# Ending the second threshold search after eight rounds behind a test, with a general path on VectorE alone; transposes of the search's bounds on VectorE; four blocks to one PSUM bank in the first expert's first rows

## The chip, the cores and the metric

One Trainium2 chip, and on it one NeuronCore (core 0). The metric is the time of one execution in device microseconds (us), taken as the median of several runs. The engines are named as the profile names them: PE (TensorE, matrix products; PEld is its weight load), DVE (VectorE), ACT (ScalarE), POOL (GpSimd) and SP (SyncE, which here only starts DMAs). They run side by side. Each works through its own list of instructions strictly in order, and they wait for each other by semaphores, so an instruction that waits holds up everything behind it on its engine.

## The reference

Attention with a block-causal mask over 8 batches, 8 heads, 576 positions and 64 dimensions gives a matrix of 4608 tokens by 512. A mixture of experts follows. Its assignment is greedy over all (token, expert) pairs, the largest logit first, and every expert takes exactly `cap` = 576 tokens:

```python
logits = x @ w_gate                      # 4608 x 8
order = np.argsort(-logits.flatten())
for idx in order:
    tok, e = (int(idx) // E, int(idx) % E)
    if assigned[tok] >= 0 or counts[e] >= cap:
        continue
    assigned[tok] = e
    counts[e] += 1
...
for e in range(E):
    mask = assigned == e
    h = np.maximum(x[mask] @ w1[e], 0.0)  # 512 -> 1024
    out[mask] = h @ w2[e]                 # 1024 -> 512
```

## The kernel before

The program has two phases. Attention fills the first 337 us and leaves the tokens in DRAM (`x`, as two float16 parts) and the logits in SBUF. Then the experts follow one after the other, in the order in which they fill up.

**The search.** `route(k)` finds the k-th expert to fill up and its 576 tokens. For each expert that is left it looks for the threshold above which 576 of the tokens that prefer it lie, and the expert with the highest threshold wins. The search runs for all experts at once, in base 4: in round t three candidates lie `4.0**-t` apart above the bound `lo` that is known so far. Two are counted on DVE (L800, L801, `jk`), one on ACT (L770, `ja`, by the sum of signs). A small matmul with a 0/1 matrix (`bo`, L817, `tot`) adds the counts over the partitions. DVE compares the sums with 4608 - 576 = 4032 (L820, `sg`) and so gets the step `nw`, and from it the next candidates (L793, `cd`). There are `NS` = 14 rounds. At round `NSC` = 6 the values are shifted into a second buffer `P2` (L774, tile `m_P`), so that the last rounds search in a small remainder. Each round therefore goes DVE and ACT, then PE, then DVE.

For k = 0 the search already ends after `NX` = 4 rounds, with a test on exactness (L868 to L897): where exactly 4032 values lie below the winner's bound the remaining rounds change nothing. The general path stands behind an If (L958) in which PE, ACT, DVE and SP all branch.

`finish()` turns the bounds (column 0, 1 and their sum 2 of `CB`), which lie one expert to a partition, into rows: three float32 transposes on PE (L831 `th`, L832 `bc`, PSUM tiles of the tags "tot" and "rt"). Then DVE finds the maximum and the winner `oh` (L835 to L845), the mask `MM` of its tokens (L849 to L861) and the expert's number `eidx` (L858). `place()` adds up the masks into positions: DVE scans (L892, `SC`), PE multiplies (L903 to L907, `po`), and `invert()` makes the index list `ix` from it (PE `pe` L1005 and `ps` L1012, DVE `ixt` L1008 and `ix` L1014).

**What hangs on a search.** `eidx` lets SP load the expert's weights (`weights`, L1018, tile `raw`, 512 KB each). They are split into two float16 parts: for k < 2 the first four pieces by ACT (L1035) and DVE (L1037), all others by ACT (L1042, L1046) and POOL (L1048). `ix` lets POOL gather the token rows (`gather`, L1078, `xg`). For k = 0 they are turned by PE (L1089, `xt`) and evicted by DVE and ACT halves (L1094, L1093); for all others SP starts transposing DMAs (L1104, tile `X`).

**An expert.** `ffn(k)` has two stages on PE. The first one (`h`, L1129) makes 8 blocks of 128 hidden units, each from 12 matmuls (4 parts of the 512 inputs by 3 products of float16 parts), for the first rows (128 of 576 for k = 0, 256 otherwise) and then for the rest. Each block fills one of the four PSUM banks of the tag "g"; ACT evicts it (L1115, `HH`) and DVE makes the remainder (L1117, `HL`), and only then the bank is free. The second stage (`y`, L1155, L1159) multiplies by the second weights; ACT evicts (L1137, `yo`), and POOL scatters the rows to the output (L1145, `out_dram`). The tag "g" serves `y` too.

**What sets the order.** All of this is written by generators that a small scheduler (`Sched`) interleaves when the program is built: each `yield` names an engine, a cost in ns and the events it needs, and the scheduler picks what starts first by its own model. So a changed cost or event moves instructions on every engine from there on. The search of expert k + 1 thereby runs beside the matmuls of expert k, its `tot` matmuls strewn among `h` and `y`. `sc.busy(e, t)` tells the model that an engine is busy, `sc.ev[...]` when an event will be there.

## Time and profile before

| | us |
|---|---|
| median of 3 runs | 771.02 (770.09 to 771.24) |
| the profiled execution | 771.09 |
| its span, first to last instruction | 769.3 |
| mean granted PE clock over the span | 0.986 |

The profiled execution takes 1.8 us more than its span; that part lies outside the first and last instruction. The page lists for each engine how long it was busy, the chain of waits that ended last, and the groups of instructions by line. Answers of the trace narrow this to a stretch of time: rows of one instruction or a merged run of them with start, duration, engine, line, operation, output and input, and in brackets how long the engine stood idle before and for whom. Durations of matmuls overlap, because they are pipelined; how long one costs is the distance from start to start.

### The profile page before, as it was taken

What the parts mean: (1) busy time and instruction counts of PE and PEld (TensorE: products, weight loads), DVE (VectorE), ACT (ScalarE), POOL (GpSimd) and SP (SyncE); (2) the same over time, 40 slices, a digit from 0 to 9 for tenths busy, and PEclk for the clock granted to TensorE, in tenths of its full rate; (3) what the DMA queues carried; (4) which work ended last, traced back from release to release, by engine and by line L of the source; (5) the groups of instructions that cost most, each with busy time, mean ns of one, the idle gap of its engine ahead of it and who ended that gap; (6) DMA issues with size and microseconds to landing.
All of it is one profiled execution on the core that took longest, in us unless ns stands there. A gap on an engine that the chain in (4) does not pass through costs nothing.

```text
span 769.3 us, 19008 instructions
## 1 busy us (share of the span) xinstructions
PE 715.6 (93%) x6516; PEld 474.7 (62%) x6516; DVE 559.4 (73%) x2290; ACT 536.6 (70%) x1451; POOL 467.8 (61%) x515
## 2 busy tenths in 40 slices
PE   5879999999999999966999999999999999999997
PEld 3557776766776777743545747647567475574753
DVE  6899889997799888758988978879687693430210
ACT  5788888988898898844935869594965948393211
POOL 5888978997799876714314448293761926666001
PEclk9999999999999999986999999999999999999999
DMA  9888999999999995266229376482925719853101
GB/s 203 163 160 171 207 187 216 201 168 226 187 210 171 221 196 103 78 124 192 99 74 228 104 247 158 161 211 71 292 76 193 178 43 268 273 139 88 35 14 49
DMA packets 249122, 122.84 MB, mean 160 GB/s; under 512 B 205600, under 2 KB 232096, under 8 KB 249024
## 3 DMA queue, kind: packets, MB, share of 16 engines
q1 hardware_dynamic: 243088, 102.60, 60.2%
q0 software_dynamic: 5936, 19.01, 7.9%
q8 instruction: 52, 0.85, 0.5%
q14 instruction: 46, 0.38, 0.2%
HBM read 71.45 MB, written 18.87 MB: 117 GB/s over the span
## 4 chain that ended last, share of the span: by engine, by line
PE 40%; DMA 5%; issue 4%; POOL 3%; ACT 1%; POOLq 0%; SPq 0%; DVE 0%; ACTq 0%; DVEq 0%
PE h L1129 22%; PE y L1155 15%; DMA raw<-in_moe_w_dram 2%; PE y L1159 2%; POOL xg L1078 2%; POOL W L1048 1%; DMA X<-xg 1%; DMA out_dram<-yo,ix 1%; PE pe L1005 1%; ACT ja L770 1%; DMA xg<-x,ix 0%; PE tot L817 0%; ACT yo L1137 0%; POOL out_dram L1145 0%; ACT raw L1042 0%
## 5 line engine op out<-in xcount | busy, mean ns | idle before, releaser
L442 POOL TENSOR_TENSOR P<-P,m 128x320 f32<-128x320 f32 (+8 forms) x285 | 210.2, 773 | 46.0 <-DVE m L434 30.6
L1129 PE MATMUL h<-X,W 128*128 128x320 f16 (+3 forms) x1536 | 195.4, 286 | 1.6 <-DMA X<-xg 1.6
L1129 PEld LDWEIGHTS <-W 128*128 128x128 f16 x1536 | 141.5, 98 | 43.1 <-issue 3.7
L420 ACT ACTIVATE P<-psb,m 128x576 f32<-128x576 f32 (+8 forms) x288 | 149.7, 548 | 25.6 <-DVE m L413 17.7
L1155 PE MATMUL y<-W,HH 128*128 128x512 f16 x512 | 152.3, 379 | 0.0
L409 DVE TENSOR_REDUCE m<-psb 128x1 f32<-128x576 f32 (+8 forms) x288 | 124.9, 481 | 11.6 <-PE psb L384 11.3
L1048 POOL TENSOR_TENSOR W<-raw,W 128x1024 f16<-128x1024 f32 x56 | 118.3, 2134 | 19.7 <-ACT W L1046 17.3
L467 PE MATMUL psb<-mident,P 128*128 128x128 f32 x800 | 104.6, 278 | 10.4 <-POOL P L442 5.4
L1145 POOL DMA_INDIRECT out_dram<-yo,ix x40 | 39.2, 981 | 118.0 <-ACT yo L1137 73.0
L384 PEld LDWEIGHTS <-qT 128*64 128x64 f16 x1408 | 77.0, 111 | 42.3 <-issue 28.0
L384 PE MATMUL psb<-kT,qT 128*64 128x288 f16 (+8 forms) x704 | 90.8, 284 | 10.8 <-ACT P L420 9.5
L467 PEld LDWEIGHTS psb<-mident,P 128*128 128x128 f32 x800 | 86.3, 141 | 22.0 <-POOL P L442 8.2
L502 PE MATMUL psb<-PT,V 128*64 128x448 f32 (+5 forms) x776 | 97.2, 388 | 0.9 <-DVE PT L450 0.4
L1155 PE MATMUL y<-W,HL 128*128 128x512 f16 x256 | 97.0, 379 | 0.0
L1115 ACT ACTIVATE HH<-h 128x320 f16<-128x320 f32 (+3 forms) x128 | 52.0, 410 | 62.3 <-PE h L1129 57.1
L1078 POOL DMA_INDIRECT xg<-x,ix x40 | 40.9, 1022 | 81.4 <-DMA raw<-in_moe_w_dram 48.5
L448 ACT ACTIVATE PT<-psb 128x512 f32<-128x512 f32 (+1 forms) x165 | 82.7, 595 | 5.3 <-PE psb L467 5.0
L1117 DVE SCALAR_TENSOR_TENSOR HL<-h,HH 128x320 f16<-128x320 f32 (+3 forms) x128 | 57.3, 452 | 37.0 <-ACT HH L1115 36.6
L384 PE MATMUL psb<-kS,qT 128*64 128x288 f16 (+8 forms) x704 | 83.2, 281 | 0.4 <-DVE kS L354 0.2
L1155 PEld LDWEIGHTS <-HH 128*128 128x128 f16 x512 | 46.9, 98 | 52.9 <-issue 1.8
L1042 ACT ACTIVATE raw<-raw 128x512 f32<-128x512 f32 x112 | 67.7, 625 | 9.4 <-DMA raw<-in_moe_w_dram 9.4
L502 PEld LDWEIGHTS psb<-PT,V 128*64 128x64 f32 x776 | 49.5, 137 | 32.2 <-issue 24.3
(241 smaller groups left out, 1035.3 us busy)
## 6 DMA issues: line engine op xcount, KB each, us to landing
raw<-in_moe_w_dram SPq DMA_DIRECT2D x64, 512.0 KB, 5.3
x<-XR SPq DMA_DIRECT2D x8, 1152.0 KB, 5.6
kn<-in_k_dram SPq DMA_DIRECT2D x15, 576.0 KB, 5.0
qn<-in_q_dram SPq DMA_DIRECT2D x15, 576.0 KB, 7.2
V<-in_v_dram SPq DMA_DIRECT2D x64, 128.0 KB, 4.1
V<-in_v_dram SPq DMA_DIRECT2D x16, 64.0 KB, 3.6
xg<-x,ix POOLq DMA_INDIRECT x41, 4.5
out_dram<-yo,ix POOLq DMA_INDIRECT x40, 2.8
```

What stands on the lines that cost most here:

```text
L384: nc.tensor.matmul(out if len(K1.shape) == 2 else out.rearrange("p (r j) -> p r j", r=2), lhsT=A[:, h, 64 * i:64 * i + 64], rhs=K1, start= ...
L409: nc.vector.tensor_reduce(m[:, 0, c:c + 1], ps[:, o:o + 64 * (i + 1)] if g else s.part(ps, g, i, o), axis=AX.X if g else AX.XY, op=OP.max)
L420: nc.scalar.activation(out, in_, AF.Exp, bias=m[:, 1, c:c + 1], scale=s.ESC, accum_out=m[:, 2, c:c + 1])
L442: nc.gpsimd.tensor_tensor(sl, sl, m[:, 3, c:c + 1].to_broadcast([P, w]), op=OP.mult)
L448: s.nc.scalar.activation(out, in_, AF.Copy)
L467: nc.tensor.transpose(ps[:, a], s.Pb[n % s.NP][:, s.OFF[i] + 128 * j:s.OFF[i] + 128 * j + P], s.ident)
L502: nc.tensor.matmul(ps[64 * h:64 * h + 64, 64 * (i0 - b0):64 * (b1 - b0)], lhsT=vn[:, j, 2 * (n % 2) + h, :], rhs=pt[:, s.PTI[(j, i0)]:s.PT ...
L1042: nc.scalar.activation(raw[:,x],raw[:,x],AF.Copy,scale=s.WS)
L1048: nc.gpsimd.tensor_tensor(lw,raw,hi,op=OP.subtract)
L1117: nc.vector.scalar_tensor_tensor(HL[:,f,ts],ps,0.0,HH[:,f,ts],op0=OP.max,op1=OP.subtract)
L1129: nc.tensor.matmul(ps,lhsT=W[:,a,d,f*P:f*P+P],rhs=X[:,4*(d//2)+d%2+l,ts],start=(d==0 and n==0),stop=(d==3 and n==2))
L1155: if m<4: nc.tensor.matmul(ps,lhsT=Z[:,f,m*P:m*P+P],rhs=Y[:,a,f],start=(f==n==0),stop=(f==7 and n==2))
```

## The change

Five things are changed.

- **The second search (k = 1) ends behind a test after round eight** (`s.EX={1:8}`, rounds 0 to 7). `early()` counts once more below the reached bound (`jx`, `cx`), adds it up on PE (`wn`), and tests whether a single expert has the highest bound and exactly 4032 values lie below it. The result is loaded into a register of DVE, and DVE alone branches. Where the test fails, `general()` does the other six rounds on DVE alone, with 32 by 32 transposes in place of the matmuls, and the heads again. For k = 1 the shift into `P2` at round 6 is left out of the live rounds.
- **The heads of all searches k > 0**: the bounds are brought into rows by three 32-wide transposes on DVE (`th3`) in place of the three on PE. For k = 0 the general path keeps PE's.
- **The first expert's first 128 rows**: four blocks of hidden units share one PSUM bank (`nf=4` for both halves of the 8 blocks), in the order of the input parts, with one eviction of 512 columns on ACT and one on DVE in place of four of 128. Only the first matmul of a bank has the start flag.
- **The times of the first expert's gathers** in the scheduler's model: cost on POOL (1350, 1300, 1900, 2000, 1750) ns in place of 1350 each, and landing after (3700, 2900, 2350, 2400, 2600) ns in place of 3000 each.
- **Order**: with these costs the scheduler places the instructions anew from the first expert on, on all engines.

```diff
-        s.NS=14; s.NSC=6; s.NX=4
+        s.NS=14; s.NSC=6; s.NX=4; s.EX={1:8}
...
-                    P2=s.P2 if t==s.NSC else None
+                    P2=s.P2 if t==s.NSC and not (live and k in s.EX) else None
...
+            def heads():
+                if k:
+                    th=rp.tile([P,3,32],F32,tag="th3",name=f"th{k}"); s.th3=th
+                    yield D,300
+                    for i in (2,0,1): V.transpose(th[:,i],CB[:,i:i+1].to_broadcast([P,32]))
+                    pb,th=th[:,0:2,0:8],th[:,2,0:8]
+                else:
...
+            def general():
...
+                for t in range(s.EX[k],s.NS):
...
+                    for i in range(3):
...
+                        V.tensor_scalar(cd,lo,(i+1)*4.0**-t,None,op0=OP.add)
+                        V.tensor_scalar(jk,PBx[:,:N],cd,0.0,op0=OP.is_lt,op1=OP.add,accum_out=z[:,i:i+1])
+                    V.transpose(zt,z)
+                    V.tensor_reduce(rs,zt.rearrange("p (a e) -> p e a",e=8),axis=AX.X,op=OP.add)
+                    for b in range(4): V.tensor_copy(s4[:,b],rs[32*b:32*b+32])
+                    V.tensor_reduce(s1,s4.rearrange("p b e -> p e b"),axis=AX.X,op=OP.add)
+                    for b in range(4): V.tensor_copy(x[32*b:32*b+32].rearrange("p (a e) -> p a e",e=8),s1[:,None,:].to_broadcast([32,4,8]))
+                    V.transpose(tt,x)
...
+            def early():
+                yield D,70
+                V.tensor_scalar(CB[:,2:3],lo,nw,None,op0=OP.add)
+                yield D,429
...
+                V.tensor_scalar(jk,PB[:,:N],CB[:,2:3],0.0,op0=OP.is_lt,op1=OP.add,accum_out=cx)
+                V.tensor_scalar(lo,lo,nw,None,op0=OP.add)
+                yield T,60
...
+                nc.tensor.matmul(wn,lhsT=cx.to_broadcast([P,P]),rhs=s.bo[:,0:8],start=True,stop=True)
+                yield from heads()
...
+                yield D,250
+                V.tensor_scalar(u8,s.th3[:,2,0:8],m1[:,0:1],0.0,op0=OP.is_equal,op1=OP.add,accum_out=n1[:,0:1])
+                V.tensor_scalar(u8,oh,n1[:,0:1],1.0,op0=OP.mult,op1=OP.is_equal)
+                yield D,90
+                V.scalar_tensor_tensor(u8,wn,float(s.NT-s.CAP),u8,op0=OP.is_equal,op1=OP.mult,accum_out=n1[:,1:2])
...
+                more=s.tc.If(rv==0,preferred_fallthrough_block=False); more.__enter__()
+                general()
+                more.__exit__(None,None,None)
+                sc.busy(D,1500)
...
-                yield from rounds(0,s.NS,True)
+                yield from rounds(0,s.EX.get(k,s.NS),True)
...
-            yield G,1038 if k else 1350,('ffn',k-2),('xm',k-1,m)
+            yield G,1038 if k else (1350,1300,1900,2000,1750)[m],('ffn',k-2),('xm',k-1,m)
...
-            if k==0: sc.ev['xg',k,m]=sc.now+3000
+            if k==0: sc.ev['xg',k,m]=sc.now+(3700,2900,2350,2400,2600)[m]
...
-                nf=4 if k==0 and h==0 and f0==0 else 1
+                nf=1 if k or h else 4
...
-                    if d==0: gk=sc.gtake(); pg[f]=s.ps.tile([P,512],F32,tag="g",name=f"h{k}_{f}_{h}",bufs=4)[:,:w],gk
+                    if new: gk=sc.gtake(); pf=s.ps.tile([P,512],F32,tag="g",name=f"h{k}_{f}_{h}",bufs=4)[:,:nf*w].rearrange("p (f t) -> p f t",f=nf)
```

Three places in the order of the instructions matter below. Names: a tile's name, its expert or round, and a running number; lines are those of each kernel.

On ACT, at the opening of the first expert, before:

```order
L770 ACTIVATE ja_1_5873,cn_1_5845<-m_PB,cd_1_5846 128x324
L1093 ACTIVATE X_5764<-xt_3_5892 128x4x128
L1093 ACTIVATE X_5764<-xt_4_5916 128x4x64
L1042 ACTIVATE raw_512_0_5851<-raw_512_0_5851 128x512
L1115 ACTIVATE HH_5849<-h_0_0_5853 128x128
L770 ACTIVATE ja_2_5955,cn_2_5947<-m_PB,cd_2_5948 128x324
L1115 ACTIVATE HH_5849<-h_1_0_5878 128x128
```

The same place now:

```order
L770 ACTIVATE ja_1_5864,cn_1_5832<-m_PB,cd_1_5833 128x324
L1150 ACTIVATE X_5764<-xt_3_5888 128x4x128
L1150 ACTIVATE X_5764<-xt_4_5931 128x4x64
L770 ACTIVATE ja_2_5943,cn_2_5929<-m_PB,cd_2_5930 128x324
L1099 ACTIVATE raw_512_0_5873<-raw_512_0_5873 128x512
L1172 ACTIVATE HH_5859<-h_0_0_5869 128x4x128
```

Round 2's count `ja_2` has moved ahead of the weight piece `raw_512_0` and of the eviction of `h`.

On DVE, the end of the second search now: from the heads to the winner's mask. The rows between the two branches, which the fast case jumps over (110 instructions of `general()`), are left out.

```order
L827 STREAM_TRANSPOSE th_6203<-CB_5791 128x32 x3
L838 TENSOR_REDUCE m_5804<-th_6203 128x1
...
L1174 SCALAR_TENSOR_TENSOR HL_5860<-h_4_1_6180,HH_5859 128x448
L888 SCALAR_TENSOR_TENSOR x_6225,x_6226<-wn_6201,x_6225 128x8
L890 TENSOR_LOAD x_6226
L894 COMPARE_AND_BRANCH
L894 UNCONDITIONAL_BRANCH
...
L906 TENSOR_TENSOR sm_6424<-m_BC_660,f_5803 128x32
L907 TENSOR_TENSOR d_1_5805<-PV_5771,f_5803 128x288
L1174 SCALAR_TENSOR_TENSOR HL_5860<-h_5_1_6211,HH_5859 128x448
```

All of these stand beside the last blocks of the first expert's `h`; the loading of the register and the branches are new on DVE at this place.

On PE, where the second search's positions (`po`) are made, before (weight loads left out, a "..." for matmuls of the same tile):

```order
L1155 MATMUL y_0_6340<-W_0_5763,HL_5850 128x512
L831 MATMUL th_6386<-mident,CB_5791 128x32
L832 MATMUL bc_6385<-mident,CB_5791 128x32 x2
L1155 MATMUL y_0_6340<-W_0_5763,HH_5849 128x512
...
L903 MATMUL po_2_6449<-m_sh,m_ones 128x72
```

and now:

```order
L1187 MATMUL h_7_1_6445<-X_5764,W_0_5762 128x448
...
L960 MATMUL po_2_6487<-m_sh,m_ones 128x72
...
L961 MATMUL po_2_6487<-MM_5767,m_tri 128x72
...
L962 MATMUL po_2_6487<-SC_5768,m_ones 128x72
...
L1213 MATMUL y_0_6492<-W_0_5763,HH_5859 128x512
```

`po` has moved from the middle of `y_1` (12 groups of three matmuls into the second stage) to the seam between the last `h` and the first `y`; `th` and `bc` are gone from PE. On every engine but DVE one UNCONDITIONAL_BRANCH (line 894) marks the place of the new If.

More of the change, by code (lines that the diff above doesn't have):

```diff
@@ L837, in finish @@
                 V.scalar_tensor_tensor(f[:,0],th,m1[:,0:1],s.wt8,op0=OP.is_equal,op1=OP.mult)
[L838 to L841 removed]
+                if k: V.tensor_copy(BC[:,0:2],pb); V.tensor_scalar(BC[:,2],pb[:,1],4.0**(1-s.NS),None,op0=OP.add)
+                else: V.tensor_scalar(BC[:,0:2],pb,s.gr,None,op0=OP.mult); V.tensor_scalar(BC[:,2],pb[:,1],s.gr,4.0**(1-s.NS),op0=OP.mult,op1=OP.add); sc.set(tk)
                 yield D,77
@@ L845, in finish @@
                 V.tensor_scalar(oh,f[:,0],m1[:,1:2],None,op0=OP.is_equal)
+            def general():
+                z,zt,rs,x,tt=[rp.tile([P,w],F32,name=f"{n}_g{k}",bufs=1) for n,w in (("z",32),("zt",32),("rs",8),("x",32),("tt",32))]
+                s4=rp.tile([32,4,8],F32,name=f"s4_g{k}",bufs=1); s1=rp.tile([32,8],F32,name=f"s1_g{k}",bufs=1)
+                lo,PBx=CB[:,0:1],PB
+                V.memset(z,0.0); V.memset(CB[:,1:2],0.0)
+                for t in range(s.EX[k],s.NS):
+                    if t==10:
+                        V.tensor_scalar(CB[:,2:3],lo,-1.0,None,op0=OP.mult)
+                        V.tensor_scalar(s.P2[:,:N],PB[:,:N],CB[:,2:3],None,op0=OP.add)
+                        lo,PBx=CB[:,1:2],s.P2
+                    for i in range(3):
+                        cd=rp.tile([P,1],F32,name=f"cd_g{k}_{t}_{i}",tag="cdg"); jk=rp.tile([P,N],F16,tag="jk",name=f"jkg{k}_{t}_{i}")
+                        V.tensor_scalar(cd,lo,(i+1)*4.0**-t,None,op0=OP.add)
[6 more added lines that the diff above has]
+                    V.transpose(tt,x)
+                    sg=rp.tile([P,4],F32,tag="sg",name=f"sgg{k}_{t}")
+                    V.scalar_tensor_tensor(sg[:,0:3],tt[:,:3],s.NT-s.CAP+0.5,s.wk[:,t:t+1].to_broadcast([P,3]),op0=OP.is_le,op1=OP.mult,accum_out=sg[:,3:4])
+                    V.tensor_scalar(lo,lo,sg[:,3:4],None,op0=OP.add)
+                V.tensor_scalar(CB[:,2:3],CB[:,0:1],CB[:,1:2],None,op0=OP.add)
+                for _ in heads(): pass
@@ L846, in finish @@
+            def finish():
+                if k in s.EX: yield from early()
+                else:
+                    yield D,140
+                    V.tensor_scalar(CB[:,2:3],CB[:,2:3],nw,None,op0=OP.add)
+                    V.tensor_scalar(lo,lo,nw,None,op0=OP.add)
+                    yield from heads()
                 sm=rp.tile([P,4,8],F32,tag="sm",name=f"sm{k}")
@@ L1111, in ffn, with hev @@
         HH=fp.tile([P,8,576],F16,tag="HH",name=f"HH{k}",bufs=1); HL=fp.tile([P,8,576],F16,tag="HL",name=f"HL{k}",bufs=1)
-        def hev(f,h,ps,gk,ts):
-            w=ts.stop-ts.start
+        def hev(f,h,ps,gk,ts,nf):
+            w=nf*(ts.stop-ts.start); x=slice(f,f+nf)
             yield A,51+.835*w
-            nc.scalar.activation(HH[:,f,ts],ps,AF.Relu)
+            nc.scalar.activation(HH[:,x,ts],ps,AF.Relu)
             yield D,69+1.042*w
-            nc.vector.scalar_tensor_tensor(HL[:,f,ts],ps,0.0,HH[:,f,ts],op0=OP.max,op1=OP.subtract)
-            sc.set(('h',k,8*h+f)); sc.set(gk)
+            nc.vector.scalar_tensor_tensor(HL[:,x,ts],ps,0.0,HH[:,x,ts],op0=OP.max,op1=OP.subtract)
+            for i in range(f,f+nf): sc.set(('h',k,8*h+i))
+            sc.set(gk)
         for h,ts in enumerate((slice(0,256),slice(256,576)) if k else (slice(0,128),slice(128,576))):
@@ L1121, in ffn @@
             for f0 in range(0,8,4):
-                pg={}
-                nf=4 if k==0 and h==0 and f0==0 else 1
+                nf=1 if k or h else 4
                 for f,d in [(f,d) for a in range(f0,f0+4,nf) for d in range(4) for f in range(a,a+nf)]:
-                    yield T,3*(w/2.4+3),'g' if d==0 else None,('g2',k-1),*[('xm',k,m) for m in range(1,5) if h],('wc',k,d) if k==0 else None
-                    if d==0: gk=sc.gtake(); pg[f]=s.ps.tile([P,512],F32,tag="g",name=f"h{k}_{f}_{h}",bufs=4)[:,:w],gk
-                    ps,gk=pg[f]
+                    new=d==0 and (f-f0)%nf==0
+                    yield T,3*(w/2.4+3),'g' if new else None,('g2',k-1),*[('xm',k,m) for m in range(1,5) if h],('wc',k,d) if k==0 else None
+                    if new: gk=sc.gtake(); pf=s.ps.tile([P,512],F32,tag="g",name=f"h{k}_{f}_{h}",bufs=4)[:,:nf*w].rearrange("p (f t) -> p f t",f=nf)
+                    ps=pf[:,(f-f0)%nf]
                     for n,(a,l) in enumerate(((0,0),(0,2),(1,0))):
-                        nc.tensor.matmul(ps,lhsT=W[:,a,d,f*P:f*P+P],rhs=X[:,4*(d//2)+d%2+l,ts],start=(d==0 and n==0),stop=(d==3 and n==2))
+                        nc.tensor.matmul(ps,lhsT=W[:,a,d,f*P:f*P+P],rhs=X[:,4*(d//2)+d%2+l,ts],start=(new and n==0),stop=(d==3 and n==2 and (f-f0+1)%nf==0))
                     sc.nolat()
-                    if d==3: sc.add(hev(f,h,ps,gk,ts),1,sc.now+200)
+                    if d==3 and (f-f0+1)%nf==0: sc.add(hev(f-nf+1,h,pf,gk,ts,nf),1,sc.now+200)
         sca=1.0/(s.XS*s.WS*s.WS)
```

28 lines of the change are left out of this document (13 added, 15 removed).

## The prediction, made before the run

> **What bounds the kernel now.** I begin with the page, then cut the span into stages, then ask in each stage what PE waited for.
>
> ```profile
> span 769.3 us, 19008 instructions
> PE 715.6 (93%) x6516; PEld 474.7 (62%) x6516; DVE 559.4 (73%) x2290; ACT 536.6 (70%) x1451; POOL 467.8 (61%) x515
> ```
>
> PE is busy for 93% of the span, so time can come from work taken off PE, or from the 54 us in which it stands. The table by stage (busy time of each engine, then the granted clock, the DMA share and GB/s) says where these lie:
>
> ```profile
> 338.00:360.00 22.00, 10.11 (x79) 4.66 (x80) 19.00 (x92) 8.74 (x17) 7.69 (x10) 0.61 0.70 210
> ...
> 370.00:418.50 48.50, 46.95 (x325) 23.49 (x322) 42.91 (x216) 30.08 (x71) 17.26 (x12) 1.00 0.39 102
> 418.50:757.00 338.50, 337.35 (x2520) 209.33 (x2521) 203.34 (x998) 210.82 (x492) 171.60 (x116) 1.00 0.52 149
> ```
>
> The largest hole (12 us, 338 to 360, the first search) is not touched: up to the first gather nothing changes. From 418.5 to 757 PE is busy for 337.35 of 338.5 us, so there only PE's own work counts. In between, the list of PE's waits (total, times, longest) for 354 to 418.6 begins:
>
> ```profile
> PE xt L1089 <- DMA xg<-x,ix: 2.3, 2, 1.9
> PE h L1129 <- DMA X<-xg: 1.6, 1, 1.6
> ...
> PE tot L817 <- DVE jk L801: 0.7, 1, 0.7
> PE tot L817 <- ACT ja L770: 0.6, 1, 0.6
> ```
>
> The first, 2.3 us for the first expert's gathers, stays: the gathers are issued as before. The three others can go.
>
> **1. The opening of the first expert.** PE's rows there:
>
> ```profile
> 364.64 0.62 PE L1089 MATMUL xt<-m_idh,xg 128*128 128x128 f16 x8 [1.88 <-DMA xg<-x,ix]
> ...
> 367.27 0.18 PE L817 MATMUL tot<-cn,m_bo 128*128 128x3 f16 x1 [0.73 <-DVE jk L801]
> 367.31 1.33 PE L1129 MATMUL h<-X,W 128*128 128x128 f16 x21
> 369.29 0.16 PE L817 MATMUL tot<-cn,m_bo 128*128 128x3 f16 x1 [0.64 <-ACT ja L770]
> ```
>
> The sums of rounds 1 and 2 stand in PE's list before their counts are there, and `h` stands behind them. The second wait comes from ACT's list, as the chain of waits shows:
>
> ```profile
> 363.01 4.80 DMA raw<-in_moe_w_dram
> ...
> 367.89 0.31 ACT raw L1042
> ...
> 368.69 0.56 ACT ja L770 x2
> ```
>
> `ja_2` was queued behind a weight piece that landed at 367.8. Now it stands ahead of it. What is late next is the eviction of `xt_3`, whose half on DVE ran right behind ACT's:
>
> ```profile
> 365.93 0.42 DVE L1094 COPY X<-xt 128x512 f16<-128x512 f16 x1 [1.65 <-ACT X L1093]
> ```
>
> I place the new list with the old durations. Both kernels have done 12 matmuls of `h` when `xt_3` starts at 364.64. DVE: `xt_3` to 366.3, `sg_1`, three `cd`, half of `jk`, `xt_4`, the other half, to 368.05. ACT's half of `xt_4` now waits for DVE's (367.6), so `ja_2` runs from 368.15 to 368.75, and `tot_2` starts at about 368.95. By then 57 matmuls of `h` are done. Before, 48 were done at 369.29, and nine more take 0.5 us (21 in 1.33): 57 at 369.87. **Gain 0.9 us.** The bounds are 0.3 (if the new wait is as long as the two together, less the nine) and 1.6 (no wait at all).
>
> The four-block bank itself I cost at nothing for PE: it has as many matmuls, and its eviction lies beside the second bank's matmuls (48 in 2.8 us). The nearest row for 512 columns:
>
> ```profile
> 391.46 0.61 DVE L1117 SCALAR_TENSOR_TENSOR HL<-h,HH 128x448 f16<-128x448 f32 x1
> ```
>
> About 0.7 us, once per 2.8 us. Without that cover a late eviction would cost at most the same 0.7 us, once, since two of the four banks are still free then.
>
> **2. The wait for the second expert's rows.** How its end hangs on the search:
>
> ```profile
> 390.82 0.59 PE L1155 MATMUL y<-W,HH 128*128 128x512 f16 x2
> ...
> 399.18 0.20 PE L903 MATMUL po<-m_sh,m_ones 128*128 128x72 f16 x1
> ...
> 404.62 0.16 DVE L1014 CAST ix<-ps 128x5 int32<-128x5 f32 x1
> ...
> 406.35 0.96 POOL L1078 DMA_INDIRECT xg<-x,ix  x1 [0.30 <-PE rt L760]
> ...
> 418.51 1.80 PE L1129 MATMUL h<-X,W 128*128 128x256 f16 x15 [1.56 <-DMA X<-xg]
> ```
>
> The first block needs the first two gathers; from the second one (406.35) to `h` it takes 12.2 us. Now six rounds are left out. `po` comes at the seam of `h` and `y`, about 389.6 (390.82 before, less what part 1 and the missing sums give). Behind `po` came `ix` after 5.4 us (399.18 to 404.62); now `pe` stands six groups of `y` (3.9 us) behind `po`, so I take 6.3 us: `ix` at 396, nine us earlier. POOL then puts a scatter (1.0 us) between the first two gathers: second gather at 398.2, rows there at 410.4. PE ends the first expert's `y` 26.1 us after the seam (390.82 to 416.95 before), at 415.7. So the rows are there 5 us ahead, and **1.56 us go**. The weights start with `eidx`, also nine us earlier.
>
> **3. Less work on PE.** Each search from k = 1 to 6 had three float32 transposes among the matmuls (k = 0 has them in its general path alone, k = 7 has no search):
>
> ```profile
> 438.19 2.20 PE L1129 MATMUL h<-X,W 128*128 128x320 f16 x15
> 440.25 0.18 PE L817 MATMUL tot<-cn,m_bo 128*128 128x3 f16 x1
> 440.29 1.38 PE L1129 MATMUL h<-X,W 128*128 128x320 f16 x9
> 441.61 0.24 PE L831 MATMUL th<-mident,CB 32*128 32x32 f32 x1
> ...
> 441.89 0.99 PE L1129 MATMUL h<-X,W 128*128 128x320 f16 x6
> ```
>
> 15 matmuls of `h` from 438.19 to 440.25 are 0.137 us apart. Nine from 440.29 end at 441.52, and the next starts at 441.89: 0.37 us for the three transposes. Six searches: **2.2 us**. By the modelled ends it would be 0.28 (441.89 less 441.61), together 1.7; that is the lower bound, the upper is 2.4. PE is full there, so all of it counts, if no other wait takes its place. On DVE the three new ones cost what L762's did:
>
> ```profile
> L762 DVE STREAM_TRANSPOSE m_PB<-PV x6: 200/207/212, 356.5 to 595.5; 128x32 f32<-128x32 f32 x6
> ```
>
> Three, overlapped, 0.45 to 0.6 us, in place of the way over PE (0.40 us idle at 395.27, hidden by a `HL` elsewhere). DVE is busy for 60% in that stage, so this is covered; without cover it is the next search that ends 0.2 us later, not PE.
>
> The six sums fall away and `wn` comes: from start to start a sum costs 0.03 us (440.25 to 440.29), five fewer are **0.15 us**.
>
> **4. What the test adds.** On PE `po` now waits for DVE's `SC` with all of `y` behind it, so DVE's way from `tot_7` to `SC` must fit into the four blocks of `h` between, 2.29 us each by the chain of waits, 9.2 us. That row, and those for DVE's way:
>
> ```profile
> 385.24 2.29 PE h L1129 x12
> ...
> L801 DVE TENSOR_SCALAR_CACHE_REDUCE jk<-m_PB,cd 128x288 f16<-128x288 f32 x20 | 9.4, 509 | 0.0
> ...
> 395.27 0.17 DVE L835 TENSOR_REDUCE m<-th 128x1 f32<-128x8 f32 x1 [0.40 <-PE th L831]
> ...
> 397.95 0.35 DVE L892 TENSOR_TENSOR_SCAN SC<-m_ones,MM 128x36 f16<-128x36 f16 x2
> ...
> L975 DVEq TENSOR_LOAD <-m x1: 544/544/544, 351.6 to 351.6; - x1
> ...
> L962 DVEq COMPARE_BRANCH  x2: 51/53/55, 354.5 to 354.8; - x2
> ...
> 355.38 0.46 DVE L754 TENSOR_TENSOR m_nP<-L,m_vm 128x288 f32<-128x288 f32 x1 [0.74 <-DVEq L962]
> ```
>
> Sum and bounds 0.6, `jx` and `lo` 0.6, transposes 0.5, heads and mask up to `SC` 3.05 (395.27 to 398.3), three tests 0.75 (as small steps of the heads), register 0.54 and its semaphores 0.2, the branches with the idle time behind them 0.74, four `HL` between 2.1 (0.53 apart). Together 9.1 us, and 0.2 us on to PE. That just fits: I take **0.2 us** of wait, between nothing and 1.5 us. Behind `po`, `pe` has 3.9 us for DVE's 3.3, so nothing waits there.
>
> The other engines each get one unconditional branch. In the first If PE took its two branches so:
>
> ```profile
> 354.88 1.89 PE L978 MATMUL warm<-m_iom,m_ones 128*128 128x512 f16 x4 [0.46 <-PEq L962]
> ```
>
> So between 0 and 0.46 us; there is one branch now, and matmuls are queued behind PE's sequencer, so I take **0.1 us**. The scheduler's new times for the gathers are no instruction of their own; their effect is part 1.
>
> **Sum.** 771.09 (the profiled execution: 769.3 of span and 1.8 around it) − 0.9 − 1.56 − 2.2 − 0.15 + 0.2 + 0.1 = 766.58, that is **766.6 us**. The profiled execution stands 0.07 above the median of 771.02, which I leave. Up to 0.2% (1.5 us) I call no change, about what a measurement of this kernel can tell.
>
> **Rivals.**
>
> *The general path runs.* Then DVE does six more rounds: per round three `cd` and `jk` (2.0 us), two transposes, two reductions, eight small copies and two small steps (some 1.9 us by rows of 0.1 to 0.2 us), 3.9 us, in all 23 us and 2 for the heads and the shift. PE would stand at `po` nearly as long, +25 us: **791 us**. It decides at the test: exactly 4032 values below the winner's bound, which is a multiple of 4^-7 = 0.000061. From the reference's inputs, worked out in double precision: the second expert to fill is number 2, its 576th candidate lies at 0.2945636 and the 577th at 0.2945484 (scaled by 32, as the search does), and the bound is 0.2945557 between them. So the test holds, but by 0.0000073; an error of that size in the chip's logits, 2.5 parts in 100,000, would fail it. 7%.
>
> *The branch stalls on its code.* The first If left 0.53 us between DVE's last branch (354.8) and its next instruction, after a jump over 97 instructions; the new one jumps over 110. [...] 10%.
>
> *The opening keeps its stall* (another late count, or a bank): only parts 2 to 4, 767.5 us. 10%.
>
> *Weights come late in the steady stage.* There PE already waits at times for a count behind a weight piece on ACT:
>
> ```profile
> PE tot L817 <- ACT ja L770: 0.8, 2, 0.7
> ```
>
> (PE's waits from 418 to 757, beside the one above.) The new order shifts all these queues. Such a wait in each of four experts is 4 × 0.7 = 2.8 us: 769.4 us. Against it: every search now ends earlier relative to the matmuls that use it. 11%.
>
> **Chances and range.** Forecast 62% (765.0 to 767.9 alone, from the bounds of parts 1, 3 and 4), the rivals as given. The last one gives about half of its chance to "within 0.2%" (769.5 to 772.6). Faster by over 0.2%: 88%; within: 5%; slower by over 0.2%: 7%. The range runs from 764.8 (all upper gains, no wait at `po`, and the 0.8 us of steady waits gone) to 769.1, leaving out the general path and the worst of late weights.
>
> **What would show it.** Right: no row of PE waiting for `X<-xg` near 416; `h` of the second expert starting near 415.7; no `jkg` row; no `th` on PE; the round sum `tot_1` without a wait and `tot_2` with up to 0.8 us; `po` directly behind the last `h`, with a wait for DVE under 1.5 us. Wrong: rows of `general()` on DVE; a gap on DVE of 2 us and more behind line 894; PE's busy time lower by less than 1.7 us; new waits of PE after 420 of over 1 us in all.

## The result: slower, 801.46 us

The kernel after the change takes 801.46 us (799.92 to 803.56, four runs), the kernel before 771.13 us beside it: a ratio of **1.039** with a 95% interval of 1.036 to 1.042. The prediction was 766.6, so it is 34.9 us off, and on the wrong side.

The page of the profile after, first its span and the busy time of each engine:

```profile
span 799.3 us, 18919 instructions
PE 720.1 (90%) x6493; PEld 475.9 (60%) x6493; DVE 587.3 (73%) x2247; ACT 533.9 (67%) x1432; POOL 466.5 (58%) x515
```

PE executes 23 matmuls fewer than before and yet is busy 4.5 us longer, and it stands for 79 us where it stood for 54. DVE executes 43 instructions fewer and is busy 28 us longer: something on DVE has become long. PE's waits from 354 us on (total, times, longest) name it:

```profile
PE rt L760 <- DVE PV L756: 22.6, 3, 7.6
PE tot L817 <- ACT ja L770: 3.5, 2, 3.1
...
PE po L962 <- DVE SC L949: 0.6, 1, 0.6
```

The first row is new. `PV` (L756) holds the values that the next search works on; DVE makes it from `m_nP` (L754) at the start of `route(k)`, and PE transposes it (`rt`) in the middle of the matmuls of expert k - 1. The two instructions in the kernel before, by groups (count, busy us, mean ns):

```profile
L756 DVE SCALAR_TENSOR_TENSOR PV<-m_nP,L 128x288 f32<-128x288 f32 x6 | 2.7, 458 | 0.2
...
L754 DVE TENSOR_TENSOR m_nP<-L,m_vm 128x288 f32<-128x288 f32 x6 | 2.7, 456 | 0.8 <-DVEq L962 0.7
```

and the same two after, as the views of these lines have them (shortest, median and longest in ns):

```profile
L754 DVE TENSOR_TENSOR m_nP<-L,m_vm x6: 448/458/9206, 357.8 to 615.1; 128x288 f32<-128x288 f32 x6
L756 DVE SCALAR_TENSOR_TENSOR PV<-m_nP,L x6: 451/457/8867, 358.4 to 624.4; 128x288 f32<-128x288 f32 x6
```

The median is what it was; three of the twelve take 8.8 to 9.2 us in place of 0.46. The timeline after shows what stands beside one of them (start, duration; in brackets the idle time before it and for whom):

```profile
550.47 0.16 DVE L1071 CAST ix<-ps 128x5 int32<-128x5 f32 x1 [0.88 <-PE ps L1069]
...
555.97 0.92 POOL L1135 DMA_INDIRECT xg<-x,ix  x1 [0.30 <-issue]
556.81 8.78 DVE L754 TENSOR_TENSOR m_nP<-L,m_vm 128x288 f32<-128x288 f32 x1
556.91 8.35 POOL L1105 TENSOR_TENSOR W<-raw,W 128x1024 f16<-128x1024 f32 x4
565.62 0.46 DVE L756 SCALAR_TENSOR_TENSOR PV<-m_nP,L 128x288 f32<-128x288 f32 x1
566.13 0.69 PE L760 MATMUL rt<-mident,PV 128*128 128x128 f32 x2 [7.57 <-DVE PV L756]
```

`m_nP` ends at 565.59, 0.33 us behind the end (565.26) of four subtractions of weight pieces that POOL does without a gap. Both inputs of `m_nP` lie in SBUF. PE stands meanwhile with `y` behind `rt`. The same place one expert later before the change:

```profile
591.43 0.17 DVE L1014 CAST ix<-ps 128x5 int32<-128x5 f32 x1 [0.89 <-PE ps L1012]
...
594.08 0.46 DVE L754 TENSOR_TENSOR m_nP<-L,m_vm 128x288 f32<-128x288 f32 x1
594.57 0.46 DVE L756 SCALAR_TENSOR_TENSOR PV<-m_nP,L 128x288 f32<-128x288 f32 x1
...
597.85 4.23 POOL L1048 TENSOR_TENSOR W<-raw,W 128x1024 f16<-128x1024 f32 x2
```

There the pair is through 3.6 us after `ix` and POOL's row starts 6.4 us after `ix`, behind the five gathers. After the change `m_nP` comes 6.34 us after `ix` and meets the row. In the windows (span, then PE, PEld, DVE, ACT, POOL busy, granted clock, DMA share, GB/s) a hole of PE is followed by a lower clock:

```profile
540.00:560.00 20.00, 18.56 (x174) 12.83 (x172) 14.57 (x45) 12.81 (x28) 7.85 (x7) 1.00 0.74 233
560.00:580.00 20.00, 13.87 (x63) 6.29 (x64) 15.37 (x61) 12.24 (x30) 12.63 (x7) 0.83 0.45 110
```

Windows of 2 us show that the clock is still low when PE, from 566.13 on, works again:

```profile
566.00:568.00 2.00, 1.86 (x6) 0.98 (x7) 1.37 (x11) 1.14 (x3) 0.00 (x0) 0.50 0.90 190
568.00:570.00 2.00, 2.00 (x9) 0.80 (x8) 0.23 (x2) 1.86 (x5) 0.00 (x0) 0.67 0.00 0
570.00:572.00 2.00, 2.00 (x13) 0.93 (x11) 1.62 (x10) 1.24 (x4) 0.00 (x0) 1.00 0.00 0
```

So a hole costs more than its length. PE's busy time in such windows times the part of the clock that is missing gives 2.6, 1.6 and 2.9 us behind the three holes, 7.1 us in all (an estimate from windows like these). On the two pages, first before and then after, the largest group of matmuls:

```profile
L1155 PE MATMUL y<-W,HH 128*128 128x512 f16 x512 | 152.3, 379 | 0.0
```

```profile
L1213 PE MATMUL y<-W,HH 128*128 128x512 f16 x512 | 156.9, 389 | 0.0
```

With the 2.3 us of the `HL` half (97.0 to 99.3) `y` is 6.9 us slower. **The bill.** From the start of the search (`sc_ps`, L710) to the end of the span lie 430.8 us before (769.3 less 338.51) and 458.3 after (799.3 less 340.97): 27.5 us more. The attention ahead of it is not touched; it was 2.46 us later in this execution. Up to the second expert's first block (`h` with 256 columns) the change gains: 80.0 us before (418.51) and 76.6 after (417.54). So behind it 30.9 us are lost: 22.6 of waits for `PV`, 3.1 for one late `ja`, 6.9 of slower `y`, 32.6 in all, less what the change takes off PE there. The 6.9 us of slower `y` are about the 7.1 us of the estimate.

### The profile page after: what moved, and what is told of

The parts are those of the page before. It is cut to its first block, busy times and chain, and to the rows that moved or that the text cites. A ratio compares the mean times of both kernels' runs of the same rounds, so it can differ in the third digit from the quotient of the medians.

```text
span 799.3 us, 18919 instructions
## 1 busy us (share of the span) xinstructions
PE 720.1 (90%) x6493; PEld 475.9 (60%) x6493; DVE 587.3 (73%) x2247; ACT 533.9 (67%) x1432; POOL 466.5 (58%) x515
## 4 chain that ended last, share of the span: by engine, by line
PE 36%; DVE 8%; DMA 2%; ACT 2%; issue 2%; POOL 1%; POOLq 0%; SPq 0%; DVEq 0%; ACTq 0%
PE y L1213 18%; PE h L1187 15%; DVE m_nP L754 2%; PE y L1217 2%; DMA raw<-in_moe_w_dram 1%; DVE PV L756 1%; DVE HL L1174 1%; DVE jk L801 1%; ACT raw L1099 1%; DMA xg<-x,ix 1%; PE pe L1062 1%; ACT W L1103 1%; POOL xg L1135 1%; ACT HH L1172 0%; DVE cd L793 0%
## 5 line engine op out<-in xcount | busy, mean ns | idle before, releaser
L1213 PE MATMUL y<-W,HH 128*128 128x512 f16 x512 | 156.9, 389 | 0.0
L467 PEld LDWEIGHTS psb<-mident,P 128*128 128x128 f32 x800 | 87.9, 142 | 24.3 <-POOL P L442 8.7
L1213 PE MATMUL y<-W,HL 128*128 128x512 f16 x256 | 99.3, 388 | 0.0
L1172 ACT ACTIVATE HH<-h 128x256 f16<-128x256 f32 (+3 forms) x122 | 51.4, 421 | 68.2 <-PE h L1187 61.0
L1174 DVE SCALAR_TENSOR_TENSOR HL<-h,HH 128x256 f16<-128x256 f32 (+3 forms) x122 | 56.4, 465 | 46.9 <-ACT HH L1172 46.7
L384 PE MATMUL psb<-kS,qT 128*64 128x288 f16 (+8 forms) x704 | 81.5, 277 | 0.4 <-DVE kS L354 0.2
L1103 ACT ACTIVATE W<-raw 128x512 f16<-128x512 f32 x112 | 68.7, 624 | 0.0
```

The costliest lines, as they stand in the source:

```text
L384: nc.tensor.matmul(out if len(K1.shape) == 2 else out.rearrange("p (r j) -> p r j", r=2), lhsT=A[:, h, 64 * i:64 * i + 64], rhs=K1, start= ...
L467: nc.tensor.transpose(ps[:, a], s.Pb[n % s.NP][:, s.OFF[i] + 128 * j:s.OFF[i] + 128 * j + P], s.ident)
L1103: nc.scalar.activation(hi[:,x],raw[:,x],AF.Copy)
L1213: if m<4: nc.tensor.matmul(ps,lhsT=Z[:,f,m*P:m*P+P],rhs=Y[:,a,f],start=(f==n==0),stop=(f==7 and n==2))
```

## The experiments

**Theory 1**: DVE instructions with two inputs in SBUF are held while POOL works off a row of subtractions of weights, and the change moves `m_nP` and `PV` under POOL's row. Only these two are pinned: `route(k)` begins with the event `('mid',k-2)`, the seam of `h` and `y`, while the searches and all that hangs on them come earlier. **Rivals**: the weights come late in the steady stage (the fourth rival of the prediction), or the transposes on DVE do it by themselves. Chips differ (the kernel before took 770.3 to 778.5 us on them), so a run is compared with the kernel before on its own chip.

| run | kernel | ratio to before, 95% interval | PE's wait `rt` for `PV` | longest `m_nP` or `PV` |
|---|---|---|---|---|
| | the change | 1.0391 (1.0359 to 1.0424) | 22.6 us | 9.21 us |
| e1 | change, `PV` early | 0.999 (0.9963 to 1.0017) | none | 0.46 |
| e3 | change without the test | 1.0094 (1.0048 to 1.0141) | none | 2.31 |
| e4 | change, transposes on PE | 1.0006 (0.998 to 1.0033) | none | 0.46 |
| e7 | before, a row of POOL added | one run, 803.88 us | 7.6 us | 8.12 |
| e11 | change, a drain on POOL | 1.0205 (1.016 to 1.0249) | none | 0.46 |
| e6 | e1 with two more planner edits | 0.9963 (0.9942 to 0.9984) | none | 0.46 |
| e8 | before, e6's three edits | 1.003 (1.001 to 1.0051) | none | 0.46 |
| e9 | e6 without the test | 1.0012 (0.9993 to 1.0032) | none | 0.46 |
| e10 | e6, transposes on PE | 0.9976 (0.9964 to 0.9989) | none | 0.46 |

The kernel before itself, run once more, took 772.22 us in its profiled execution. It met a chip of 771 us, so what makes another chip take 778 us stays open.

> The kernel before, unchanged, for its profile on the chip on which the other runs of this call are made. On the chip of the first runs it took 778 us, against 771 us on the chip of the first profiles, and two kernels without the long VectorE instructions came out level with it. If the difference between the chips is one of late weights and gathers, PE waits longer than 4 us in all at `tot` and `X<-xg` here; if it is one of PE's clock, the granted clock shows it.

### e1: make PV early

```diff
-        yield D,369 if k>1 else 30,('Lm',k),('mid',k-2)
+        yield D,369 if k>1 else 30,('Lm',k),('mid',k-2) if last else None
...
-                yield T,214,'rt'
+                yield T,214,'rt',('mid',k-2)
```

> The changed kernel; only the planner's condition that holds the next search's first three VectorE steps (vm, m_nP, PV) back until the second half of the FFN of two experts before has begun is moved behind PV, to the PE transposes `rt`. No instruction is added or left out. Theory 1 (VectorE instructions with two SBUF inputs are held for as long as GpSimd runs its row of weight subtractions, and m_nP or PV starts just as that row begins): m_nP and PV now run before the gathers, none of them lasts over 1 us, the three waits of PE at `rt` (22.6 us) and the lower clock behind them go; 801.5 minus 22.6 minus some 7 to 10 us of matmuls at the lower clock = 768 to 773, or less if the wait for `ja` (3.1 us) goes too. Theory 2 (what the change itself adds to VectorE costs the time: the test, the branch past the general path, the transposes): nothing of that is touched, 795 to 803. Theory 3 (the weights are late in every later expert, and `rt` only hides it): 775 to 790, with new waits of PE on the weights or on the converted rows.

Ratio 0.999: **nearly all of the loss is gone** with one event moved (the scheduler places other instructions anew with it). PE's waits that are left:

```profile
PE tot L817 <- ACT ja L770: 7.4, 4, 2.7
PE tot L817 <- DVE jk L801: 2.9, 3, 2.4
```

No `rt`, and no row of POOL shorter than before: this speaks for the place of the two instructions, and e11 below tests it with the order kept. But nothing is gained either, since 10 us of new waits for counts stand where the change took work off PE. That is the prediction's fourth rival, as a smaller part.

### e3 and e4: which half of the change moves the order

e3 sets `s.EX={}` (no early test), e4 gives the searches k > 0 their three transposes on PE back in the live path.

> The changed kernel without the test behind round eight (all searches make 14 rounds; no branch, no general path); the three transposes on VectorE and the four blocks to one PSUM bank stay. Theory 1: the searches end later against the FFN than in the changed kernel, two or three HL steps instead of four stand between a search's end and m_nP, so m_nP and PV end before GpSimd's row begins: no VectorE instruction over 4 us, 766 to 772. Theory 2 in the form that the transposes on VectorE cost it (every search has them): 790 or more. Theory 2 in the form that the test and its branch cost it: 766 to 772 as well; this run and the next tell these apart only together.

> The changed kernel with the test behind round eight, its branch and its general path, but with the border values again by PE transposes into PSUM in the six later searches (on VectorE only inside the general path). Theory 1: two or three HL steps stand between a search's end and m_nP, not four; no instruction over 4 us, or one at most; 766 to 776. Theory 2 with the test, the branch or the code behind it as the cost: 795 or more, since all of that is there. `f` reads `th` from PSUM here, so by theory 1 it is back from 2.17 and 1.60 us to about 0.23 us; by a cost of the code behind the branch it stays long.

Neither has a long `m_nP`. e4 came as expected: what is left of the change makes no difference. But it was close: with the test alone the pair comes 4.1 to 5.4 us behind `ix`, and twice `PV` ends 0.3 us before POOL's row begins. e3 missed: it is 0.9% slower for another reason, which its waits show,

```profile
PE tot L817 <- ACT ja L770: 5.1, 5, 1.5
PE h L1187 <- POOL W L1105: 3.8, 1, 3.8
```

and its window:

```profile
460.00:480.00 20.00, 12.14 (x76) 7.04 (x77) 11.24 (x66) 14.74 (x36) 13.45 (x9) 0.83 0.71 138
```

Here weights are late, for one expert, with a hole of nearly 8 us on PE. In these runs it took test and transposes together to bring the three pairs under the row, and an order can go wrong in more than one place.

### m1 and m2: the hold by itself

Two kernels of their own run four of POOL's subtractions back to back beside six DVE instructions of one kind: `o<-a,b` with both inputs in SBUF, one with an input in PSUM, a count with accumulator, transposes, copies. In m1 the subtractions write one tile, in m2 one each.

> A kernel of its own that leaves out the reference's computation (its output is zeros): in 15 stretches GpSimd runs a row of 0, 1, 4 or 8 subtractions of the size of the weights' (128x1024), and VectorE, released just behind it, six instructions of one kind. Theory 1: with two inputs in SBUF (m_nP's, PV's and OL's forms, and the small one of 8 elements) the first of the six lasts until the whole row has ended, some 2, 8.4 and 16.8 us for 1, 4 and 8 subtractions, the other five their usual 0.46 us; with one input in PSUM, or with one tensor input (the search's sums), all six last as without GpSimd. Theory 2: no instruction is longer than without GpSimd by over 0.2 us. Open: whether a gap or a small memset between GpSimd's instructions lets VectorE in, whether a GpSimd instruction with one input holds it too, and whether VectorE, when first, holds GpSimd.

> A kernel of its own as the first of this kind (it leaves out the reference's computation, its output is zeros), but each of GpSimd's subtractions in a row now writes a tile of its own, as in the kernels studied; in the first one they all wrote the same tile, and a held VectorE instruction lasted 2.26 us, one subtraction's time and its own, not the row's. [...] Theory 1b (VectorE gets in between any two GpSimd instructions): 2.3 us whatever the row, and the 8.4 to 9.2 us of the changed kernel have another cause.

The view of m2's line with two SBUF inputs:

```profile
L46 DVE SCALAR_TENSOR_TENSOR o<-a,b x6: 457/2256/2259, 29.8 to 39.5; 128x288 f32<-128x288 f32 x6
```

Without POOL it is 0.46 us. Beside POOL it takes 2.26 us, once for each subtraction: the length of **one** and not of the row, so the expectation of m1 (8.4 us for four) missed and the first form of the theory fell. Beside a row in m1, six instructions with an input from PSUM took 0.457 us in the mean, six counts 0.51 and six transposes 0.21: these are untouched. Two inputs are not a condition, though: copies of one float32 tile took 1.54 us in the mean of six in m1, and up to 2.16 in place of 0.31. The 8.8 to 9.2 us of the changed kernel are four times the 2.26, and neither of the two kernels shows why.

### e7: a row of POOL in the kernel before

Four additions of 128 x 1024 that read `vm` were put on POOL behind `vm` of the fourth to seventh search; the order of DVE and PE stays that of before.

```diff
+        if 2<k<E-1:
...
+            for i in range(4): nc.gpsimd.tensor_tensor(s.dum[:,i],s.dui,vm[:,0:1].to_broadcast([P,1024]),op=OP.add)
```

> The kernel before, with four GpSimd additions of 128x1024 on scratch tiles put behind `vm` of each search from the fourth to the seventh, the first of them reading vm, so that they start together with m_nP. Nothing is changed on VectorE. Theory 1: m_nP (or PV) lasts some 8 us in each of the four searches instead of 0.46 us, and PE waits for PV at `rt` about 5 to 8 us each time; 790 to 815 us, beside what the gathers lose that stand behind the row in GpSimd's queue. Rival (a row of GpSimd instructions alone does no such thing; the changed kernel's VectorE stream is slow for another reason): m_nP and PV stay at 0.46 us, and the time within 5 us of before.

Of four expected long holds one came. Rows of its timeline at two of the searches:

```profile
504.45 7.93 POOL L741 TENSOR_TENSOR dum<-dui,m_vm 128x1024 f16<-128x1024 f32 x4 [13.94 <-DVE SC L745]
...
504.90 2.03 DVE L759 SCALAR_TENSOR_TENSOR PV<-m_nP,L 128x288 f32<-128x288 f32 x1
...
559.99 0.96 POOL L1081 DMA_INDIRECT xg<-x,ix  x1 [0.30 <-issue]
...
560.61 8.12 DVE L759 SCALAR_TENSOR_TENSOR PV<-m_nP,L 128x288 f32<-128x288 f32 x1
560.96 7.44 POOL L741 TENSOR_TENSOR dum<-dui,m_vm 128x1024 f16<-128x1024 f32 x4
```

The row that POOL began from rest held `PV` for one instruction (2.03 us). The row that stood **directly behind a gather** held it to the row's end (8.12 us), and so did all three in the changed kernel (8.78 to 9.21 us). In the one that it met at 619.86 `PV` was through before. (The time itself proves little: the rows also delay gathers, with 6.4 us of wait for `X`, and 12.9 for `ja`.)

### m3 and m4: a gather ahead of the row

m3 puts one gather, three or none ahead of no, one or four subtractions and lets three DVE instructions start at several moments; m4 puts a small instruction between gather and row.

> A kernel of its own (it leaves out the reference's computation, its output is zeros). In the two kernels of this kind so far a row of four subtractions let VectorE in between any two of them (2.26 us at most); in the studied kernels the row held m_nP, PV or SC to its end (8.1 to 9.2 us), and in four of five such cases a gather stood right ahead of the row on GpSimd. Here 22 stretches run none, one or three gathers, then none, one or four subtractions, with three two-input instructions of VectorE released at steps of 0.2 us across the gather. [...] Theory 1d (the gather doesn't matter; what differs is something else of the studied kernels): 2.3 us in every stretch.

> A kernel of its own (it leaves out the reference's computation, its output is zeros): one gather, then one small thing on GpSimd, then four subtractions, with three two-input instructions of VectorE released 0.6 to 1.4 us behind the flag, so that one of them meets the gather. Between gather and row stands nothing, a memset of one column, a memset of 1024 columns, an instruction that reads one column, a drain, or an instruction that waits for ScalarE for over 1 us. [...] If the gather changes how GpSimd runs all that comes later, until it has stood idle, only the wait ends it, and the others give 9 us.

Three places of m3's line of DVE instructions: a gather and four subtractions, a gather and one, no gather and four.

```profile
L62 DVE SCALAR_TENSOR_TENSOR o<-a,b x3: 457/457/9059, 58.9 to 59.8; 128x288 f32<-128x288 f32 x3
...
L62 DVE SCALAR_TENSOR_TENSOR o<-a,b x4: 457/482/2974, 114.5 to 120.9; 128x288 f32<-128x288 f32 x4
...
L62 DVE SCALAR_TENSOR_TENSOR o<-a,b x3: 458/2257/2258, 241.9 to 244.6; 128x288 f32<-128x288 f32 x3
```

**9.06 us with a gather directly ahead of the row, 2.26 without.** So theory 1d, with 2.3 us in every stretch, missed. The held instruction started some 0.4 us before POOL's first subtraction, in the gather's last part. In m4 a memset of one column (9.09 to 9.18 us) or a read of one column (9.25 to 9.38) between gather and row did not end it; a wider memset and a drain put the row too late for DVE to meet it, and show nothing. The wait for ACT that was to part the two did not come about: ACT was done before the gather ended, and the one instruction that met the row took 9.32 us.

In m3 and m4 each instruction with the long hold began before the row, in the gather. Two more traces show that neither this nor a gather as such is needed. The first is e1's, the second that of the kernel before:

```profile
653.48 0.92 POOL L1135 DMA_INDIRECT xg<-x,ix  x1 [0.30 <-issue]
654.41 8.39 POOL L1105 TENSOR_TENSOR W<-raw,W 128x1024 f16<-128x1024 f32 x4
...
655.79 7.11 DVE L949 TENSOR_TENSOR_SCAN SC<-m_ones,MM 128x36 f16<-128x36 f16 x1
```

```profile
660.41 1.00 POOL L1145 DMA_INDIRECT out_dram<-yo,ix  x1 [0.17 <-issue]
...
661.23 4.47 DVE L921 TENSOR_SCALAR h<-q 128x36 f16<-128x36 f32 x1
661.44 4.21 POOL L1048 TENSOR_TENSOR W<-raw,W 128x1024 f16<-128x1024 f32 x2
```

`SC` (0.21 us at its shortest) began 1.38 us inside the row and was held to its end (the same in e3, 7.11 us), and `h` (0.18 us, with one input tile) was held through both subtractions of a row behind a scatter. PE did not wait for either. So theory 1 stands in this form: a DVE instruction of one of the kinds that are held, a row of POOL directly behind a gather or scatter, and the hold to the row's end (7.11 to 9.38 us with rows of four, 4.47 with the row of two, in these runs). It costs time where PE has to wait for the result.

### e11: the order kept, the gather parted from the row

```diff
+            if m==4 and k>1: nc.gpsimd.drain()
```

behind the last gather of an expert; DVE's and PE's order is that of the change.

> The changed kernel with one GpSimd drain behind the last gather of each expert from the third on, and nothing else touched: VectorE's and PE's order stay as they were. In the kernel of its own just run, a drain behind a gather took 4.6 to 5.3 us and no VectorE instruction met the row behind it; a memset or a read of one column between gather and row did not end the long hold (9.1 to 9.3 us). So the drain moves GpSimd's row away from m_nP and PV by some 4.6 us instead of moving these away from it. Theory (the meeting of the two is what costs): m_nP and PV are back at 0.46 us, PE's 22.6 us at rt and the low clock behind them go, 770 to 782, less easily below since the later weights come 4.6 us later. Rival (the cost lies in VectorE's own stream): 795 to 803. If the weights' lateness takes over: PE waits for W at h, 785 to 800.

The timeline at the first of the three places, and PE's longest sum of waits:

```profile
497.37 0.91 POOL L1135 DMA_INDIRECT xg<-x,ix  x1 [0.30 <-issue]
...
498.12 0.46 DVE L756 SCALAR_TENSOR_TENSOR PV<-m_nP,L 128x288 f32<-128x288 f32 x1
501.34 6.30 POOL L1105 TENSOR_TENSOR W<-raw,W 128x1024 f16<-128x1024 f32 x3 [3.05 <-ACT raw L1099]
```

```profile
PE tot L817 <- ACT ja L770: 17.5, 10, 5.5
```

`PV` starts in the last gather as it did in the change (there 497.14 to 506.01), and takes 0.46 us: the drain keeps the row 3 us away. The holds and the `rt` waits are gone, and half of the loss with them (1.0205 for 1.0391), **with the order of DVE and PE unchanged**. The other half missed the expectation of 770 to 782 us. The time lies in the range given for late weights (785 to 800), but PE does not wait for `W` at `h`: each row now comes 3.05 to 6.7 us later, and PE waits for counts on ACT, 17.5 us in ten places. So this run shows that the meeting costs at least half of the loss; that a row a little later than the gather would not hold is shown by m3's pair (9.06 and 2.26 us), not here.

### e6, e8, e9, e10: is there a gain, and whose

e6 is e1 with two more edits of the planner: it is told that `rt` is evicted 2 us later, and that the second expert's late weights land 3 us later, so that counts aren't put behind them.

```diff
+                if k>1: sc.lag(2000)
...
+                    if k==1 and n>3: sc.ev['wl',k,n]+=3000
```

e8 is the kernel before with the same edits, e9 is e6 without the test, e10 is e6 with transposes on PE.

> The changed kernel with m_nP and PV ahead of the gathers (as in the first run), and the planner told two things more: the first round of the later searches starts 2.0 us later behind the rows' copy, and the second expert's last weights land 3.0 us later than it thinks, so that `ja` stands ahead of their scaling on ScalarE. Theory: what was left of PE's waits there (2.7 us and 1.6 to 2.4 us four times at `tot`, 10.7 us in all) are rounds that the planner put a few us too early; with them gone the expected gain of 4 to 5 us comes out: ratio 0.985 to 0.995. Rival (weights and gathers set the pace there, and a wait taken away comes back at the next product): ratio 0.996 to 1.003, with waits of about the same sum at other places.

> The kernel before with the planner's three edits of the last timed run (m_nP and PV ahead of the gathers, 2.0 us more ahead of the first round, 3.0 us more for the second expert's last weights), and nothing of the change. It tells how much of that run's 0.37% is the planner's edits alone. If the change is worth its work (theory): 0.998 to 1.002 here, and the change's 2.6 us stand apart from them. If the edits give it (rival): 0.994 to 0.998 here too, and the change itself is worth nothing.

> The changed kernel with the planner's three edits and 14 rounds in all searches (no test, no branch, no general path). By the terms of the prediction it lacks the second expert's wait for its rows (1.56 us) and five round sums (0.15 us) and saves what the test adds (0.3 us): 1.4 us above the run with all of it, ratio 0.997 to 0.999.

> The changed kernel with the planner's three edits and the border values by PE transposes in the six later searches. By the terms of the prediction it lacks 6 times 0.37 us = 2.2 us of PE: ratio 0.998 to 1.000. If the modelled ends of the matmuls are nearer the truth than their starts, it lacks only some 0.5 us: 0.996 to 0.998. `f` stays at 0.23 us here and takes 2.17 us with VectorE's transposes.

e6 **beats the kernel before** by 0.37%, 768.88 us against 771.47. That is less than was expected (0.985 to 0.995) and in the range of its rival. But the rival's waits of the same sum did not come: PE's 10.3 us at `tot` in e1 went down to

```profile
PE tot L818 <- ACT ja L771: 1.9, 4, 0.8
```

The edits alone make the kernel before 0.3% slower (1.003), so they are not the gain. The change's own work is worth 0.37% (2.9 us) against the kernel before as it is, and about 0.67% (5 us) against the one with the same edits, which suit it less; the two ratios are from two chips. Taking away the test costs 0.5% (1.0012 to 0.9963, two chips again, and each kernel in an order of its own), some 3.8 us. Taking away the transposes on DVE costs 0.13%, 1.0 us, with intervals that overlap, so it may be nothing. e9 missed its expectation upward. e10 missed the first one (0.998 to 1.000) and fell into the one for the modelled ends of the matmuls (0.996 to 0.998).

## Why the prediction was wrong, step by step

**What failed** is the step from the first table of windows, "so there only PE's own work counts", and its twin in part 3, "PE is full there, so all of it counts, if no other wait takes its place". That PE was busy for 337.35 of 338.5 us was the state of one order, with a margin of 2.8 us that the prediction never read: 3.6 us from `ix` to the end of `PV` where the two are furthest apart, 6.4 to POOL's row. After the change `ix` of the fourth search came 8.9 us earlier (158.8 us behind `sc_ps` before, 149.9 after); the pair, pinned to its seam, came only 2.7 us earlier (158.4 and 155.7), and 5.8 to 6.3 us from `ix` to `m_nP` ate the margin. That it is mainly the test that moves `ix` is shown by e4, which has it without the transposes (153.0). e1 (the pair moved), e11 (the row kept away, the order left) and m3 (9.06 against 2.26 us) show the three links. The prediction priced every DVE instruction at its usual length, and no rival of it had a longer one: its 7% for "slower" were the general path alone. Yet the trace before had such a hold, `h` with 4.47 us in place of 0.18. Against its fourth rival the prediction held that "every search now ends earlier relative to the matmuls that use it": just this was the cause.

- **Part 1, 0.9 us.** Right in direction, and more: the seam (the first `y` before, `po` after) lies 52.3 us behind `sc_ps` before (390.82) and 50.1 after (391.03), 2.25 us earlier for the 1.2 that the seam's forecast (389.6) held. `tot_1` does not wait any more and `tot_2` for 0.33 us (370.32), as forecast.
- **Part 2, 1.56 us.** The wait for `X` is gone, and `ix` came at 398.13 for the 396 forecast, or 395.7 without the 2.46 us by which this execution was later. But e9 has no test, its `ix` comes 65.8 us behind `sc_ps` as before (66.1), and there is no such wait either: the new order was enough. So the test, to which the sum credited it, was not needed for this gain. The test's gain, 3.8 us in e6, has to lie elsewhere; where was not taken apart.
- **Part 3, 2.2 us.** Mis-sized: at most 1.0 us (e10), perhaps none. The step counted PE's 0.37 us of each search; what it missed is that `th` moves from PSUM to SBUF with it and so turns `f` (L840), covered on paper, into an instruction with two inputs in SBUF.
- **Part 4, 0.2 us at `po`.** 0.8 us of waits (0.6 for `SC`, 0.2 for `MM`), within the bounds of 0 to 1.5. The timeline after has the reason:

```profile
382.08 4.22 POOL L1105 TENSOR_TENSOR W<-raw,W 128x1024 f16<-128x1024 f32 x2 [0.40 <-ACT W L1103]
...
384.15 2.17 DVE L840 SCALAR_TENSOR_TENSOR f<-th,m,m_wt 128x8 f32<-128x8 f32 x1
...
388.97 0.19 DVE L906 TENSOR_TENSOR sm<-m_BC,f 128x32 f32<-128x32 f32 x1 [1.16 <-DVEq L894]
...
391.03 0.20 PE L960 MATMUL po<-m_sh,m_ones 128*128 128x72 f16 x1
...
392.12 0.19 PE L962 MATMUL po<-SC,m_ones 128*128 128x72 f16 x1 [0.60 <-DVE SC L949]
```

  `f` with its eight elements takes 2.17 us, until POOL's piece ends (386.30), on the very way that was said to "just fit". In e4, with `th` in PSUM, `f` takes 0.23 us.
- **The rivals.** The general path did not run: `f` and `sm` stand 5 us apart, not 28. The branch left no gap of 2 us: 1.16 us of idle time at line 894, with the register's load in it, against 0.74 at the first If. On PE `h` ran on beside it without idle time (386.30 to 391.19), so the 0.1 us taken for PE's branch does not show. Late weights came true as a small part: one row after the change,

```profile
419.93 0.63 ACT L1099 ACTIVATE raw<-raw 128x512 f32<-128x512 f32 x1 [3.38 <-DMA raw<-in_moe_w_dram]
...
421.16 0.16 PE L817 MATMUL tot<-cn,m_bo 128*128 128x3 f16 x1 [3.12 <-ACT ja L770]
```

  where a count stood 3.1 us behind a weight piece, and most of what was left over in e1 and e11. The forecast's own size, 4.5 us in sum, came close to what e6 shows against e8 (about 5), once the holds are away; against the kernel before as it is, e6 gains 2.9. With parts 2 and 3 wrong as they are, that the sum comes near is luck. The forecast's own bounds (765.0 to 767.9) are not what the bounds of its parts add up to either, 765.5 to 769.0.

## What to carry to other kernels

A change that lets one chain end earlier shifts it against everything that is pinned elsewhere: list which instructions stay where they were, and read their distance to what now moves towards them. An engine's fullness proves nothing for a new order; the margins of the old order do. Price an instruction by its longest as well as its median: here the kernel before already had one of 4.47 us, off the critical path. Where DVE reads two tiles from SBUF, look at what POOL does at that moment and what stood ahead of it: here 0.46 us became 2.26 beside a row of POOL, and 8.8 to 9.2 beside a row behind a gather.

## What the runs showed of the hardware

A DVE instruction with two SBUF inputs was held for one POOL subtraction in most meetings (2.26 us in m2, 2.03 in e7, 2.17 even for eight elements), but to the end of the whole row of four (8.1 to 9.2 us) where a gather stood directly ahead of the row, though it began up to 0.5 us before the row by the profile's times. One that began 1.38 us inside such a row was held to its end too (7.11 us in e1), and a row behind a scatter did the same (4.47 us before the change). A float32 copy with one input was held as well (up to 2.16 us in m1, 1.54 in the mean of six). Instructions with an input from PSUM, counts with accumulator and transposes were not held in m1 (0.457, 0.51 and 0.21 us in the mean). After holes of 7.5 to 8 us on PE the 20 us window in which the hole ends shows a granted clock of 0.74 to 0.83 (0.74, 0.83 and 0.74 in the changed kernel, 0.83 in e3); in windows of 2 us it was 0.50 at the hole's end and back at 1.00 some 4 to 7 us after PE had begun again (in the changed kernel). The mean matmul of `y` over the whole kernel rose from 379 to 389 ns. Why a gather or scatter prolongs the hold stays open.
